# One load of x in 16 rows, a split of the last values, and four more key rows per part on VectorE in a decode attention kernel

## The chip, the cores and the metric

The kernel runs on one core of one Trainium2 chip. The metric is device time in microseconds (us) of one execution, here the median of three. A profiled execution gives, besides its own time, a span from the first to the last instruction; what lies around the span is launch and end.

The engines by the profile's names: PE (TensorE, matmuls; PEld is its weight loads), DVE (VectorE), ACT (ScalarE), POOL (GpSimd) and SP (SyncE, which here only issues DMAs). SBUF is the on-chip memory, PSUM the memory that matmuls write to. All DMAs of the core share 16 DMA engines.

## The reference

One token (x has 512 numbers) goes through a layer norm; its result is the input of an attention over a key and value cache with 32 heads of 128 and a window of the last 4096 positions, and of a small MLP. The MLP's silu gates the attention's output. With a sequence of one, the four shifted groups in the MLP (g0 to g3) are zero. Every head has its own keys and values, so the kernel reads 32 heads x 4096 positions x 128 numbers x 2 bytes = 32 MiB of keys and as much of values, once each.

```python
def _A_ref(x, k_cache, v_cache, wq, wo):        # 32 heads of 128, window W = 4096
    q = (x @ wq).reshape(B, Sq, Hq, Dh).transpose(0, 2, 1, 3)
    k = k_cache[:, :, Sk - W:, :]
    v = v_cache[:, :, Sk - W:, :]
    scores = jnp.einsum("bhqd,bhkd->bhqk", q, k) * (Dh ** -0.5)
    o = jnp.einsum("bhqk,bhkd->bhqd", softmax(scores), v)
    return o.transpose(0, 2, 1, 3).reshape(B, Sq, Hq * Dh) @ wo

xn = layernorm(A_x)
s = _A_ref(xn, A_k_cache, A_v_cache, A_wq, A_wo)
g = silu(_B_ref(xn, B_w1, B_w2, B_w3, B_w4))    # MLP with layer norm, gelu and residual
return A_x + s * g
```

## The kernel before

**Tiling.** The heads are worked in eight groups of G = 4. A group's keys (4 MB) fill one tile of 128 partitions x 128 rows x 128 numbers (CP = 128): partition p holds 128 positions of one of the four heads. A group's values lie in the same way. There are three buffers for keys and, once the weights' pool `wts` has been given back, two for values.

**DMA order.** SP issues nearly all loads, in program order and through one queue (q1 in the profile): w2, w3, w4, then keys of groups 0 (in two halves, rows 0 to 63 and 64 to 127), 1 and 2, values of group 0, keys of 3, values of 1, and so on. Blocks of wo are in between. An issue waits until the buffer that it fills is free, and what is behind it in SP's order waits too. The last group's values come in pieces (`cuts`, L528: rows 0 to 63, 64 to 95, 96 to 127), and after them the rows of wo of the last four heads, two heads at a time (L543 to L545). x and wq are issued by ACT, on a queue of their own (q10): x twice, as 128 partitions of 4 numbers (`x_bf`, L79) and as 4 rows of 128 on partitions 0, 32, 64 and 96 (`x_row`, L82).

**Start.** x_bf is cast (L183), the layer norm follows (L158 to L179, with two matmuls by ones and a POOL power), then q (L208) as soon as wq has landed, then its spreading over the partitions (`q_bc`, L216) and its transposes (`q_pair`, L225). The MLP (L228 to L280) runs beside it; its row form uses `xn_row` (L242), which is made from x_row, and ends in `g_row`. The PSUM pool `ps_misc` has one buffer, which all tiles of the tag "misc" use in turn.

**Scores.** Each group's 128 key rows are shared out (`nd`, L308). The first nd rows go to DVE in four equal parts (`k_vector`, L316: a product with q_bc, L321, and a sum over the 128 numbers, L323). The others are transposed by PE two rows at a time (`k_turn`, L339), copied from PSUM by ACT (L342) and multiplied with q_pair (`k_scores`, L350). nd is 80, but 64 in group 0 and in group 7.

**Softmax and values.** Maximum (`sm_max`, `sm_turn`), exponential with its sum (`sm_exp`, L388), then the product with the values, four rows in one matmul (`v_wide`, L427), copy (L433), transposes (`v_turn`, L444), sum (`v_add`, L450) and scaling by the denominator (`v_out`). These run two groups behind the keys (LAG = 2). PE, DVE and ACT have an order written out by hand in this loop (from L529); each runs its instructions in that order.

**End.** For the last group, rows 0 to 95 of the values go through v_wide, v_turn and v_add; v_add writes its sum to a PSUM tile `oT`, and the 32 matmuls of `v_part` (L461) add rows 96 to 127 to the same tile. L471 scales it, the 16 matmuls of `y_head` (L525, by L155: four for each head) apply the last four heads' rows of wo, L654 multiplies with g_row, L656 adds x_row, and the result goes out. `warm` (L506) issues matmuls on zeros whose result nobody reads.

Of the kernel before, what the change touches and what calls it, by code (L numbers as in the profile page):

```python
# [8 lines left out]
P = 128  # L9
BF16 = mybir.dt.bfloat16  # L10
FP32 = mybir.dt.float32
ACT = mybir.ActivationFunctionType
ALU = mybir.AluOpType
AX = mybir.AxisListType
# [4 lines left out]
G = 4  # L19
# [3 lines left out]
LATE = 7  # L23
# [3 lines left out]
def kernel(  # L27
# [14 lines left out]
    nc = tc.nc  # L42

    Bb, Sq, D = A_x.shape
# [30 lines left out]
    def load(dst, src):  # L75
        return tc.keep_in_program_order(nc.sync.dma_start(out=dst, in_=src))  # L76

    x_bf = small.tile([P, KC], BF16, name="x_bf")
    nc.scalar.dma_start(out=x_bf[:], in_=A_x.rearrange("a b (p c) -> p (a b c)", p=P))  # L79
    x_row = small.tile([P, P], BF16, name="x_row")  # L80
    nc.gpsimd.memset(x_row[:], 0.0)
    nc.scalar.dma_start(out=x_row[0:P:32, :], in_=A_x.rearrange("a b (j n) -> (a b j) n", j=KC))  # L82
    wq_sb = wts.tile([P, KC, HD], BF16, name="wq_sb")
    nc.scalar.dma_start(out=wq_sb[:].rearrange("p c n -> p (c n)"),
                        in_=A_wq.rearrange("(a b c) n -> b a (c n)", a=4, c=KC))
# [93 lines left out]
        return xc, negmean, rstd  # L179


    x_f = small.tile([P, KC], FP32, name="x_f")
    nc.vector.tensor_copy(out=x_f[:], in_=x_bf[:])  # L183
    xc, negmean, rstd = ln_stats(x_f[:], "x")
    xn_f = small.tile([P, KC], FP32, name="xn_f")
    nc.vector.tensor_scalar(out=xn_f[:], in0=xc[:], scalar1=rstd[:], scalar2=None, op0=ALU.mult)
# [51 lines left out]
    z3_bf = small.tile([P, KC], BF16, name="z3_bf")  # L238
    nc.vector.tensor_scalar(out=z3_bf[:], in0=xc3[:], scalar1=rstd3[:], scalar2=None, op0=ALU.mult)

    xn_row = small.tile([P, P], FP32, name="xn_row")
    nc.vector.tensor_scalar(out=xn_row[:], in0=x_row[:], scalar1=negmean[:], scalar2=rstd[:],  # L242
                            op0=ALU.add, op1=ALU.mult)
# [62 lines left out]
    st = {}  # L306

    def nd(g):  # L308
        return 64 if g == 0 or g >= LATE else 80

    def k_open(g):
        st[g] = {
# [101 lines left out]
    def load_rows(h, n):  # L414
        load(wo_rows[:, h - h_part:h - h_part + n, :],
             A_wo[h * P:(h + n) * P, :].rearrange("(h p) n -> p h n", p=P))
# [28 lines left out]

    def v_add(g):
        s = st[g]
        if g < NG - 1:
            s["oT"] = sm_pool.tile([P, G], FP32, tag="oT", name="oT")
        nc.vector.tensor_reduce(out=s["oT"][:], in_=s["ot"][:].rearrange("p (x m) -> p m x", m=32)[:, 0:G, :],  # L450
                                axis=AX.X, op=ALU.add)

    def v_open(g):
        st[g]["oT"] = ps_tr.tile([P, G], FP32, tag="pt", name="oT")
        nc.tensor.matmul(st[g]["oT"][:], lhsT=zero_bf[:], rhs=zero_bf[:, 0:G], start=True, stop=False,
                         skip_group_check=True)

    def v_part(g, v, c0, c1):
        s = st[g]
        for c in range(c0, c1):  # L460
            nc.tensor.matmul(s["oT"][:], lhsT=v[:, c, :], rhs=s["pT"][:, c, :], start=False,  # L461
                             stop=(c == CP - 1), skip_group_check=True)

    def v_out(g):
        h = G * g
        b = [i for i, (h0, _) in enumerate(blocks) if h >= h0][-1]
        if b not in o_blk:
            o_blk[b] = sm_pool.tile([P, blocks[b][1]], BF16, tag=f"o{b}", bufs=1, name="o")
        c = h - blocks[b][0]
        if g >= NG - 5:  # L470
            nc.vector.tensor_tensor(out=o_blk[b][:, c:c + G], in0=st[g]["oT"][:], in1=st[g]["rden"][:],  # L471
                                    op=ALU.mult)
            return
        for k in range(G):
            nc.scalar.mul(o_blk[b][:, c + k:c + k + 1], st[g]["oT"][:, k:k + 1], st[g]["rden"][:, k:k + 1])
# [49 lines left out]
        rows_add(y_ps, o_blk[3][:, h - h_part:h - h_part + 1], wo_row(h), h == H - 1)  # L525

    NG = H // G
    cuts = (0, 64, 96, CP)  # L528
    region = tc.manual_schedule(engines={mybir.EngineType.PE, mybir.EngineType.DVE,  # L529
                                         mybir.EngineType.Activation})  # L530
    region.__enter__()
# [1 line left out]
    for s in range(NG + LAG):  # L533
# [7 lines left out]
            wo_rows = v_pool.tile([P, H - h_part, D], BF16, tag="wo_rows", bufs=1, name="wo_rows")  # L541
        if last:
            v = load_kv(v_pool, A_v_cache, h, cuts)  # L543
            for r in (H - G, H - 2):
                load_rows(r, 2)  # L545
        elif h >= 0:
            v = load_kv(v_pool, A_v_cache, h)
        if h == 3:
# [7 lines left out]
        if s < NG:  # L556
            nb = len(batches(s))

            def keys(b0, b1):
                for b in range(b0, b1):  # L560
                    k_turn(s, kn, b)
                    if b > 0:
                        k_scores(s, b - 1)

            k_open(s)
            k_vector(s, kn, 0)
            keys(0, 2)
            if s == 7:
                v_turn(h - 1)
                v_add(h - 1)  # L570
                v_out(h - 1)
            elif s > 1:
                sm_den(s - 2)
                sm_rden(s - 2)
            elif s == 1:
                sm_max(0)
            k_vector(s, kn, 1)
            keys(2, 4)
            if s == 7:
                sm_den(h)  # L580
                sm_rden(h)
                keys(4, nb - 2)
                sm_turn(s - 1)
                keys(nb - 2, nb)
            else:
                if s > 0:
                    sm_turn(s - 1)
                keys(4, nb)
            k_scores(s, nb - 1)
            sm_own(s)  # L590
            if s == 7:
                k_vector(s, kn, 2)
                v_wide(h, v)
                sm_exp(s - 1)
                v_turn(h)
                y_open()
                k_vector(s, kn, 3)
                v_add(h)
                v_out(h)
                ox_spread(1)  # L600
                sm_max(s)
                continue
            if s > 0:
                sm_exp(s - 1)
            if h > 0:
                v_turn(h - 1)
            k_vector(s, kn, 2)
            if h >= 0:
                v_wide(h, v)
            if h > 0:  # L610
                v_add(h - 1)
                v_out(h - 1)
            if s == 6:
                ox_spread(0)
            k_vector(s, kn, 3)
            if s == 6:
                ox_pick(0)
            if s > 0:
                sm_max(s)
        elif s == NG:  # L620
            ox_pick(1)
            sm_turn(NG - 1)
            sm_exp(NG - 1)
            y_wide(1, False)
            sm_den(NG - 2)
            sm_rden(NG - 2)
            y_wide(0, False)
            warm(3)
            v_wide(h, v)
            sm_den(NG - 1)  # L630
            sm_rden(NG - 1)
            v_turn(h)
            v_add(h)
            v_out(h)
            ox_spread(2)
        else:
            v_open(h)
            warm(2)
            v_wide(h, v, cuts[1], last=False)
            ox_pick(2, 1)  # L640
            y_wide(2, True)
            nc.scalar.copy(out=y_sum[:], in_=yr[0][:].rearrange("p j n -> p (j n)"))
            v_wide(h, v, cuts[2], cuts[1])
            warm(2)
            v_turn(h)
            v_add(h)
            rows_add(y_ps, ind, y_sum, False)
            v_part(h, v, cuts[2], CP)
            v_out(h)
            for r in range(H - G, H):  # L650
                y_head(r)
# [36 lines left out]
```

## Time and profile before

| what | before |
|---|---|
| three runs, us | 193.21, 193.31, 193.57 (median 193.31) |
| profiled execution, us | 193.37 |
| its span, us | 191.2 |
| PE, DVE, ACT busy in the span, us | 121.2, 150.9, 89.5 |
| read from HBM, MB | 78.84, 412 GB/s over the span |
| DMA engines' time by q1, q10, q8 (code) | 91.6%, 5.1%, 0.3% |
| granted PE clock, mean | 0.704 |
| x_bf: issue, landing | 0.74, 4.77 |
| wq: matmuls start | 19.87 |
| first DVE product on keys (group 0, group 1) | 25.93, 42.08 |
| last issue of keys, first matmul on them | 130.42, 153.51 |
| output DMA issued | 188.71 |

Times inside an execution are us from the start of its span. A row of the profile's list of groups names line, engine, operation, tiles, shapes and how often it ran, then busy us and mean ns, and behind the last bar the idle time of that engine just before it and what ended that. The chain of waits is followed back from the last instruction: each piece is the work, or the DMA, that released the next one. The windows give, for a stretch of time, the busy time (and instructions) of PE, PEld, DVE, ACT and POOL, the granted PE clock, the mean busy share of the 16 DMA engines, and GB/s. The trace also holds a record of every DMA packet and of every landing (a DMA has landed when all 16 engines have reported).

### The profile page before, as it was taken

What the parts mean: (1) busy time and instruction counts of PE and PEld (TensorE: products, weight loads), DVE (VectorE), ACT (ScalarE), POOL (GpSimd) and SP (SyncE); (2) the same over time, 40 slices, a digit from 0 to 9 for tenths busy, and PEclk for the clock granted to TensorE, in tenths of its full rate; (3) what the DMA queues carried; (4) which work ended last, traced back from release to release, by engine and by line L of the source; (5) the groups of instructions that cost most, each with busy time, mean ns of one, the idle gap of its engine ahead of it and who ended that gap; (6) DMA issues with size and microseconds to landing.
All of it is one profiled execution on the core that took longest, in us unless ns stands there. A gap on an engine that the chain in (4) does not pass through costs nothing.

```text
span 191.2 us, 2843 instructions
## 1 busy us (share of the span) xinstructions
PE 121.2 (63%) x1161; PEld 77.0 (40%) x1161; DVE 150.9 (79%) x175; ACT 89.5 (47%) x191; POOL 2.4 (1%) x11
## 2 busy tenths in 40 slices
PE   1554853989826368356945773681889289749772
PEld 0430222767615334243434432540764078513321
DVE  1560169979999999999999999999999997990111
ACT  2001270887795076527364654552575147743120
POOL 2110000000000000000000000000000000000000
PEclk9999696555665556955585579558555855996999
DMA  6999999999999999999999999999999998999990
GB/s 202 436 444 410 431 425 432 439 439 437 432 440 432 432 428 439 439 439 418 428 418 425 439 428 408 456 432 435 439 439 434 428 432 379 471 435 394 415 372 29
DMA packets 4572, 79.02 MB, mean 413 GB/s; under 512 B 624, under 2 KB 1232, under 8 KB 1488
## 3 DMA queue, kind: packets, MB, share of 16 engines
q1 hardware_dynamic: 4264, 74.65, 91.6%
q10 hardware_dynamic: 296, 4.20, 5.1%
q8 instruction: 9, 0.15, 0.3%
q14 instruction: 3, 0.02, 0.0%
HBM read 78.84 MB, written 0.00 MB: 412 GB/s over the span
## 4 chain that ended last, share of the span: by engine, by line
DVE 47%; DMA 42%; PE 6%; ACT 1%; issue 1%; SPq 1%; DVEq 0%; ACTq 0%
DMA kv<-in_A_k_cache_dram 31%; DVE S L323 28%; DVE prod L321 16%; DMA kv<-in_A_v_cache_dram 9%; PE pt L339 3%; DMA x_bf<-in_A_x_dram 2%; ACT kt L342 1%; PE ov L427 1%; PE sT L350 1%; DVE m L366 1%; SPq L76 1%; DVE S L364 1%; DVE mx L374 1%; PE oT L461 1%; PE ot_ps L444 0%
## 5 line engine op out<-in xcount | busy, mean ns | idle before, releaser
L323 DVE TENSOR_REDUCE S<-prod 128x20 f32<-128x2560 bf16 (+1 forms) x32 | 86.0, 2686 | 1.1
L342 ACT COPY kt<-pt 128x1024 bf16<-128x1024 bf16 x52 | 51.4, 1013 | 40.0 <-PE pt L339 38.1
L339 PE MATMUL pt<-ident_f,kv 128*128 128x128 f32 x208 | 49.2, 392 | 10.0 <-DMA kv<-in_A_k_cache_dram 10.0
L321 DVE TENSOR_TENSOR prod<-kv,q_bc 128x2560 bf16<-128x2560 bf16 (+1 forms) x32 | 45.4, 1417 | 3.6 <-ACT q_pair L225 1.8
L339 PEld LDWEIGHTS pt<-ident_f,kv 128*128 128x128 f32 x208 | 36.2, 205 | 13.9 <-DMA kv<-in_A_k_cache_dram 9.3
L350 PE MATMUL sT<-q_pair,kt 128*128 128x8 bf16 x416 | 19.6, 170 | 14.9 <-ACT kt L342 14.8
L350 PEld LDWEIGHTS <-kt 128*128 128x128 bf16 x416 | 16.9, 105 | 26.1 <-ACT kt L342 24.9
L427 PE MATMUL ov<-kv,pT 128*16 128x512 bf16 x248 | 23.2, 536 | 1.2 <-DMA kv<-in_A_v_cache_dram 1.2
L388 ACT ACTIVATE pT<-S,mb 128x128 bf16<-128x128 f32 x32 | 13.9, 572 | 0.3
L372 PE MATMUL mt_ps<-ident_f,m 128*1 128x128 f32 x8 | 2.9, 360 | 16.6 <-DVE rden L399 16.1
L433 ACT COPY ov_sb<-ov 128x512 f32<-128x512 f32 x8 | 4.7, 586 | 18.4 <-PE ov L427 18.4
L427 PEld LDWEIGHTS <-pT 128*16 128x16 bf16 x248 | 6.9, 112 | 14.3 <-issue 12.7
L359 ACT ACTIVATE own<-sT,par 128x48 f32<-128x48 f32 (+1 forms) x32 | 7.5, 356 | 3.7 <-PE sT L350 3.7
L444 PE MATMUL ot_ps<-ident_f,ov_sb 128*128 128x128 f32 x32 | 7.5, 379 | 2.2 <-ACT mb L384 1.7
L211 DVE CAST q_row<-qr_ps 128x512 bf16<-128x512 f32 x1 | 0.7, 692 | 10.0 <-PE qr_ps L208 10.0
L388 ACT ACTIVATION_READ_ACCUMULATOR pT<-S,mb 128x1 f32 x32 | 8.3, 258 | 0.0
L372 PEld LDWEIGHTS mt_ps<-ident_f,m 128*1 128x1 f32 x8 | 0.6, 80 | 17.1 <-DVE rden L399 16.4
L399 DVE RECIPROCAL rden<-den_ps 128x4 f32<-128x4 f32 x8 | 1.4, 175 | 6.7 <-PE den_ps L394 6.7
L381 PE MATMUL mb_ps<-md,par_t 5*128 5x4 f32 x16 | 3.9, 311 | 4.1 <-DVE md L376 4.1
L255 ACT ACTIVATE a_row<-a_ps 128x384 bf16<-128x384 f32 x1 | 0.5, 491 | 12.1 <-remote 12.1
L444 PEld LDWEIGHTS ot_ps<-ident_f,ov_sb 128*128 128x128 f32 x32 | 4.8, 188 | 3.2 <-ACT mb L384 2.1
L208 PE MATMUL qr_ps<-wq_sb,xq_bf 128*1 128x512 bf16 x32 | 3.5, 611 | 3.6 <-DMA wq_sb<-in_A_wq_dram 3.6
(122 smaller groups left out, 82.8 us busy)
## 6 DMA issues: line engine op xcount, KB each, us to landing
kv<-in_A_k_cache_dram SPq DMA_DIRECT2D x7, 4096.0 KB, 31.0
kv<-in_A_v_cache_dram SPq DMA_DIRECT2D x7, 4096.0 KB, 30.6
wq_sb<-in_A_wq_dram ACTq DMA_DIRECT2D x1, 4096.0 KB, 17.5
kv<-in_A_k_cache_dram SPq DMA_DIRECT2D x2, 2048.0 KB, 27.5
wo<-in_A_wo_dram SPq DMA_DIRECT2D x1, 2048.0 KB
kv<-in_A_v_cache_dram SPq DMA_DIRECT2D x1, 2048.0 KB
kv<-in_A_v_cache_dram SPq DMA_DIRECT2D x2, 1024.0 KB, 16.3
w_sb<-in_B_w_dram SPq DMA_DIRECT2D x1, 1376.0 KB, 10.3
```

Of the source, the lines that this page charges most:

```text
L208: nc.tensor.matmul(qr[b][32 * a:32 * a + 1], lhsT=xq_bf[:, c:c + 1], rhs=wc[:, 4 * b:4 * b + 4, a, :], start=False, stop=(c == KC - 1), sk ...
L321: nc.vector.tensor_tensor(out=prod[:, 0:m, :], in0=kn[:, rows, :], in1=q_bc[:, g:g + 1, :].to_broadcast([P, m, Dh]), op=ALU.mult)
L323: nc.vector.tensor_reduce(out=st[g]["S"][:, rows], in_=prod[:, 0:m, :], axis=AX.X, op=ALU.add)
L339: nc.tensor.transpose(pt[:, i, :], kn[:, c:c + 2, :].rearrange("p c d -> p (c d)").bitcast(FP32), ident_f[:])
L342: nc.scalar.copy(out=kts[b][:, 0:n, :], in_=pt[:, 0:n, :].bitcast(BF16))
L350: nc.tensor.matmul(st[g]["sT"][:, c:c + 2, :].rearrange("p c a -> p (c a)"), lhsT=kt[:, i, l::2], rhs=q_pair[:, g, l, :], start=(l == 0), ...
L359: nc.scalar.mul(s["own"][:, 0:m, a], s["sT"][:, 0:m, a], par[:, a:a + 1])
L381: nc.tensor.matmul(mb_ps[:], lhsT=par_t[:].rearrange("k b a -> k (b a)"), rhs=md[:], start=True, stop=True)
L388: nc.scalar.activation(out=s["pT"][:, :, a], in_=s["S"][:], func=ACT.Exp, scale=scale, bias=mb[:, a:a + 1], accum_out=s["sum"][:, a:a + 1])
L427: nc.tensor.matmul(ov[r:r + 4 * G], lhsT=s["pT"][:, c:c + 4, :].rearrange("p i a -> p (i a)"), rhs=v[:, c:c + 4, :], start=(i < 4), stop=( ...
L433: nc.scalar.copy(out=s["ov_sb"][:], in_=ov[:])
L444: nc.tensor.transpose(ot_ps[:, step * j:step * j + P], s["ov_sb"][:, j, :], ident_f[:])
```

## The change

1. x is loaded once, as 16 rows of 32 numbers (`x_in`). Both forms are made of it on chip: a matmul with a 0/1 matrix (`x_up`) copies every row to its 8 partitions, a mask (`x_own`) and a sum pick each partition's 4 numbers (`x_f`); for x_row the rows are spread by a mask (`r_in`), and a matmul with another 0/1 matrix (`r_up`) puts them together. These are 2 small matmuls and 9 small DVE instructions, in place of a cast on DVE, a memset on POOL and two DMAs (one remains).
2. In group 0, 76 key rows go to DVE rather than 64, in parts of 19 rather than 16.
3. The last 32 rows of the last values come in two halves. The matmuls on them add up in a PSUM tile of their own (`oP`); v_add's sum goes to SBUF, and one more DVE instruction (`both`) adds the two. In PE's order, the matmul rows of y_sum and the first half's 16 matmuls now stand ahead of the transposes of v_turn, and the second half's 16 behind; one call of warm(2) is gone.
4. The last four heads' rows of wo come as three heads and one, not two and two.

```diff
-    x_bf = small.tile([P, KC], BF16, name="x_bf")
-    nc.scalar.dma_start(out=x_bf[:], in_=A_x.rearrange("a b (p c) -> p (a b c)", p=P))
-    x_row = small.tile([P, P], BF16, name="x_row")
-    nc.gpsimd.memset(x_row[:], 0.0)
-    nc.scalar.dma_start(out=x_row[0:P:32, :], in_=A_x.rearrange("a b (j n) -> (a b j) n", j=KC))
+    XR, XC = 16, D // 16
+    x_in = small.tile([XR, XC], BF16, name="x_in")
+    nc.scalar.dma_start(out=x_in[:], in_=A_x.rearrange("a b (r n) -> (a b r) n", r=XR))
...
+    m8 = P // XR
+    x_up = wts.tile([XR, XR, m8], BF16, name="x_up")
+    nc.vector.tensor_copy(out=x_up[:], in_=ident_bf[0:XR, 0:XR].unsqueeze(2).to_broadcast([XR, XR, m8]))
+    x_own = wts.tile([P, m8], BF16, name="x_own")
+    nc.vector.tensor_reduce(out=x_own[:], in_=ident_bf[:].rearrange("d (i t) -> d t i", t=m8), axis=AX.X, op=ALU.max)
+    x_all = ps_misc.tile([P, m8, KC], FP32, tag="misc", name="x_all")
+    nc.tensor.matmul(x_all[:].rearrange("p t c -> p (t c)"), lhsT=x_up[:].rearrange("k r t -> k (r t)"), rhs=x_in[:],
+                     start=True, stop=True)
+    x_pick = wts.tile([P, m8, KC], FP32, name="x_pick")
+    nc.vector.tensor_tensor(out=x_pick[:], in0=x_all[:], in1=x_own[:].unsqueeze(2).to_broadcast([P, m8, KC]), op=ALU.mult)
     x_f = small.tile([P, KC], FP32, name="x_f")
-    nc.vector.tensor_copy(out=x_f[:], in_=x_bf[:])
+    nc.vector.tensor_reduce(out=x_f[:], in_=x_pick[:].rearrange("p t c -> p c t"), axis=AX.X, op=ALU.add)
...
+    r_slot = wts.tile([XR, KC], BF16, name="r_slot")
+    nc.vector.tensor_reduce(out=r_slot[:], in_=ident_bf[0:XR, 0:XR].rearrange("k (j a) -> k a j", a=KC), axis=AX.X, op=ALU.max)
+    r_row = wts.tile([XR, KC], BF16, name="r_row")
+    nc.vector.tensor_reduce(out=r_row[:], in_=ident_bf[0:XR, 0:XR].rearrange("k (j a) -> k j a", a=KC), axis=AX.X, op=ALU.max)
+    r_up = wts.tile([XR, KC, PB], BF16, name="r_up")
+    nc.vector.tensor_copy(out=r_up[:], in_=r_row[:].unsqueeze(2).to_broadcast([XR, KC, PB]))
+    r_in = wts.tile([XR, KC, XC], BF16, name="r_in")
+    nc.vector.tensor_tensor(out=r_in[:], in0=x_in[:].unsqueeze(1).to_broadcast([XR, KC, XC]),
+                            in1=r_slot[:].unsqueeze(2).to_broadcast([XR, KC, XC]), op=ALU.mult)
+    xr_ps = ps_misc.tile([P, P], FP32, tag="misc", name="xr_ps")
+    nc.tensor.matmul(xr_ps[:], lhsT=r_up[:].rearrange("k j b -> k (j b)"), rhs=r_in[:].rearrange("k a n -> k (a n)"),
+                     start=True, stop=True)
+    x_row = small.tile([P, P], BF16, name="x_row")
+    nc.vector.tensor_copy(out=x_row[:], in_=xr_ps[:])
...
     def nd(g):
-        return 64 if g == 0 or g >= LATE else 80
+        return 76 if g == 0 else 64 if g >= LATE else 80
...
     def v_add(g):
         s = st[g]
-        if g < NG - 1:
-            s["oT"] = sm_pool.tile([P, G], FP32, tag="oT", name="oT")
+        s["oT"] = sm_pool.tile([P, G], FP32, tag="oT", name="oT")
...
     def v_open(g):
-        st[g]["oT"] = ps_tr.tile([P, G], FP32, tag="pt", name="oT")
-        nc.tensor.matmul(st[g]["oT"][:], lhsT=zero_bf[:], rhs=zero_bf[:, 0:G], start=True, stop=False,
+        st[g]["oP"] = ps_tr.tile([P, G], FP32, tag="pt", name="oP")
+        nc.tensor.matmul(st[g]["oP"][:], lhsT=zero_bf[:], rhs=zero_bf[:, 0:G], start=True, stop=False,
                          skip_group_check=True)
...
+        if g == NG - 1:
+            both = sm_pool.tile([P, G], FP32, tag="both", bufs=1, name="both")
+            nc.vector.tensor_tensor(out=both[:], in0=st[g]["oP"][:], in1=st[g]["oT"][:], op=ALU.add)
+            st[g]["oT"] = both
...
-    cuts = (0, 64, 96, CP)
+    cuts = (0, 64, 96, 112, CP)
...
-            for r in (H - G, H - 2):
-                load_rows(r, 2)
+            load_rows(H - G, G - 1)
+            load_rows(H - 1, 1)
...
             v_wide(h, v, cuts[2], cuts[1])
-            warm(2)
+            rows_add(y_ps, ind, y_sum, False)
+            v_part(h, v, cuts[2], cuts[3])
             v_turn(h)
             v_add(h)
-            rows_add(y_ps, ind, y_sum, False)
-            v_part(h, v, cuts[2], CP)
+            v_part(h, v, cuts[3], CP)
             v_out(h)
```

More of the change, by code (lines that the diff above doesn't have):

```diff
@@ L460, in v_part @@
         for c in range(c0, c1):
-            nc.tensor.matmul(s["oT"][:], lhsT=v[:, c, :], rhs=s["pT"][:, c, :], start=False,
+            nc.tensor.matmul(s["oP"][:], lhsT=v[:, c, :], rhs=s["pT"][:, c, :], start=False,
                              stop=(c == CP - 1), skip_group_check=True)
```

## The prediction

> **What bounds the kernel now.** First the page's 40 slices, then the chain of waits, the windows of the last microseconds, and the rows of each operation.
>
> ```profile
> DMA  6999999999999999999999999999999998999990
> GB/s 202 436 444 410 431 425 432 439 439 437 432 440 432 432 428 439 439 439 418 428 418 425 439 428 408 456 432 435 439 439 434 428 432 379 471 435 394 415 372 29
> ...
> q8 instruction: 9, 0.15, 0.3%
> ...
> DVE 47%; DMA 42%; PE 6%; ACT 1%; issue 1%; SPq 1%; DVEq 0%; ACTq 0%
> ```
>
> The chain puts VectorE (DVE) first, but the DMA row is full from the second slice to the last but one. 78.84 MB at some 435 GB/s take 181 us of the 191.2 us span. DVE stands in the chain because it frees key buffers: the load of the last keys is issued at 130.42, when DVE has read an old buffer, and lands at 153.47. By the landings in the trace the queue still held work up to 143.7 at that moment, so an issue a few us later starts no byte later. I read the kernel as one DMA stream with a tail; a step counts if it changes the stream or the tail.
>
> The tail, in the chain:
>
> ```profile
> 168.94 17.25 DMA kv<-in_A_v_cache_dram
> ...
> 186.24 0.97 PE oT L461 x32
> ...
> 187.23 0.17 DVE o L471
> ...
> 187.45 0.59 PE y_ps L155 x16
> ...
> 188.06 0.30 DVE y L654
> ```
>
> The last values land, 32 matmuls (L461) finish their sum, DVE scales it, 16 matmuls (L155) apply the last four heads' rows of wo. But those 16 did not run through. The weight loads of that line in the timeline from 187.6 on, and the answer on the rows' tile:
>
> ```profile
> 187.73 0.10 PEld L155 LDWEIGHTS <-o 128*1 128x1 bf16 x7
> ...
> L76 SPq DMA_DIRECT2D wo_rows<-in_A_wo_dram x2: 469/531/593, 169.6 to 170.2; - x2
> ...
> DMA to landing us min/median/max: 17.3/17.4/17.5
> ```
>
> The second pair of rows was issued at 170.2 and landed 17.5 us later, at 187.7. The first 8 matmuls start by 187.51, the other 8 from 187.73. So the landing of wo_rows, not the values' sum, releases the end, and any byte ahead of it counts.
>
> ```profile
> 183.50:185.50 2.00, 1.58 (x14) 0.64 (x13) 0.00 (x0) 1.10 (x2) 0.00 (x0) 1.00 0.99 398
> 185.50:186.00 0.50, 0.50 (x11) 0.11 (x8) 0.23 (x1) 0.00 (x0) 0.00 (x0) 1.00 0.54 193
> 186.00:186.50 0.50, 0.32 (x14) 0.27 (x11) 0.00 (x0) 0.00 (x0) 0.00 (x0) 1.00 0.65 227
> 186.50:187.00 0.50, 0.50 (x26) 0.50 (x23) 0.00 (x0) 0.00 (x0) 0.00 (x0) 1.00 0.54 193
> 187.00:187.50 0.50, 0.25 (x12) 0.16 (x13) 0.16 (x1) 0.00 (x0) 0.00 (x0) 1.00 0.19 55
> ```
>
> The last two columns (DMA share, GB/s) fall to half from 185.5: some DMA engines are done, others work until 187.2. The packet records say why: a 32 KB packet takes 1.213 us, but the one after an instruction packet (the q8 row: 16 KB, some 1.07 us) takes 1.7, so its engine falls behind by about 1.55 us. Eight such packets lie inside the stream and land on different engines; these end last. The ninth starts at 187.213, right behind the last packet of the last engine (187.207), and that engine's landing came 0.48 us after its last packet, where the other late ones needed 0.29 to 0.35. I read 0.13 us of the end as that collision. In "Runtime: NRT & Kernel Launch", section "Instruction fetch mechanics", the Trainium skill says that an engine's sequencer fetches code itself in blocks of 256 instructions, with the cost mostly hidden; the records agree on the block (16 KB, one per some 130 PE pairs of load and matmul), but here it is not hidden, since DMA is the bound.
>
> **The change, part by part** (us of the span).
>
> *x once.* Now x_bf is 128 packets of 8 bytes, 8 per DMA engine, each holding its engine 15 ns (9 and a gap of 6): 0.12. x_row is four packets and one DMA more: 0.02. The new load is 16 packets, one per engine. Stream: -0.12. A larger gain is not excluded: w2's first 8 packets per engine take until 4.23, 2.45 from the first packet at 1.78, while a first packet of 1.0 and seven of 0.165 make 2.16; so -0.29 is the far bound, and 0 the near one. I take -0.12, the packets' own time. The chain names x_bf (issue 0.74, landing 4.77) because the second half of the first keys is issued behind it; that half's bytes start moving only at 20 or later, so an earlier issue is worth nothing.
>
> x_f now comes through a matmul (0.16, as L194), a product (0.21, L494) and a reduce (0.27, L498) in place of a cast of 0.17: 0.5 more, hidden by the wait for wq: xq_bf is ready at 9.05, wq at 19.87. Without that cover, +0.5. The masks x_up and x_own (0.26 and 0.38 by L192 and L136) run before x lands. Of the five row operations on DVE each lies between 0.16 (L188) and 0.41 (the pick of 256), 0.8 to 2.1 together; DVE idles 10.0 before q_row (L211). xr_ps shares the one "misc" buffer: behind it wait a_ps's zeros, at most 0.9, before w3's matmuls.
>
> wq's issue starts 1.1 earlier (x_row's 1.09 is gone). wq then shares the engines with w3 from the start, packet by packet, so w3, and with it a_ps (2.93, ahead of q on TensorE), comes later: q ends between 1.1 earlier and 0.7 later. Up to 0.5 of the earliness is lost anyway, because DVE's first product starts at 25.93 and the first keys land at 25.83. V's first issue (30.98) waits for hr; the queue has work until 51.
>
> *76 rows on DVE.* Bound by DVE's own rows:
>
> ```profile
> L323 DVE TENSOR_REDUCE S<-prod 128x20 f32<-128x2560 bf16 x24 | 67.7, 2820 | 0.8
> L321 DVE TENSOR_TENSOR prod<-kv,q_bc 128x2560 bf16<-128x2560 bf16 x24 | 35.6, 1483 | 1.7 <-DMA kv<-in_A_k_cache_dram 1.6
> L323 DVE TENSOR_REDUCE S<-prod 128x16 f32<-128x2048 bf16 x8 | 18.3, 2285 | 0.2
> L321 DVE TENSOR_TENSOR prod<-kv,q_bc 128x2048 bf16<-128x2048 bf16 x8 | 9.8, 1219 | 1.9 <-ACT q_pair L225 1.8
> ...
> 42.08 1.49 DVE L321 TENSOR_TENSOR prod<-kv,q_bc 128x2560 bf16<-128x2560 bf16 x1 [1.32 <-DMA kv<-in_A_k_cache_dram]
> ...
> 162.58 0.28 DVE L374 TENSOR_REDUCE mx<-mt_ps 1x4 f32<-1x128 f32 x1 [1.15 <-PE mt_ps L372]
> ```
>
> A row costs (1483-1219+2820-2285)/4 = 200 ns, twelve cost 2.4. The idle 1.32 before the second keys takes part, so DVE is about 1.1 late from 42 (up to 1.8 with a late q). It gets 0.33 back at 134.12 (waiting for keys) and 1.15 at 162.58 (waiting for TensorE). Its later releases delay issues at 57, 76, 94, 112 and 130, each with 10 to 20 us of work queued. Cost 0; without all that cover +2.4. ScalarE saves one copy of eight (1.0), TensorE 6 transposes and 12 score matmuls: worth nothing in time, but 18 pairs fewer in TensorE's code.
>
> *Last values in two halves.* Each DMA engine moves 16 packets of 4 KB (0.159) in place of 8 of 8 KB (0.309), with gaps of 6 ns and one semaphore packet: +0.13 of stream. SP issues one DMA more (0.55, ending at 171.2), while those bytes have their turn from 183 on. In the tail L461 has 16 matmuls behind the last landing instead of 32 (25 ns apart): -0.40; `both` adds one DVE step of 0.20. So o is ready 0.20 earlier, 187.25 for TensorE: hidden, since wo_rows decides; without that cover -0.2. The transposes (0.66) now follow the first half's 16 matmuls (landing near 185.0) and end at about 186.1, just before the last landing at 186.2. The two warm matmuls' place is taken by y_sum's rows.
>
> *Three heads and one.* The same bytes; behind the last landing stand 4 matmuls, not 8: -0.06 (187.79 to 187.73 for the last start). Three heads land 0.35 earlier, about 187.2, in time for o.
>
> *The ninth code fetch.* 18 pairs fewer and the two new matmuls against the two warm ones: the fetch comes some 18 pairs later, among the last 16 matmuls, behind the end of the stream: -0.13, or 0 if my reading of the 0.48 is wrong. I take -0.13.
>
> Sum: -0.12 +0.13 -0.06 -0.13 = -0.18. The profiled run took 193.37 (span 191.2, 2.17 around it), so 193.19; the median of the three runs, 193.31, lies 0.06 lower: **193.13**.
>
> **Rivals.** *The clock.* "TensorE: Matmul & The Clock Gate" of the Trainium skill (section "Part 1: The HAM clock gate") says that activity in a window of about 3.4 us releases the throttle and idleness brings it back; the page's PEclk agrees (0.50 in 173.7 to 177.0, 1.00 after). Two warm matmuls (0.6) go, so the tail could run at half clock: four transposes take 1.12 at half (125.53) against 0.66, the second half then starts 0.36 late, o is ready 0.15 after before's: 193.4. Against: from 180.6 to 183.8 TensorE works 1.8 of 3.2, unchanged, and keeps 1.00. 7%.
>
> *The first loads bring the stream forward.* If the chain were right that x_bf holds up the keys, the stream would move by x's earlier landing, 1.3 to 2: about 191.7. Against: the DMA row is full. 6%. A better start within the -0.29 bound gives 192.96; 15%.
>
> *DVE becomes the bound (slower).* If the 1.1 of lateness at 42 reaches the issue at 130.42 and with it the last keys' landing, as the chain links them, the time is 193.31 + 1.1 = 194.4. For it: DVE has 47% of the chain and no gap from 42 to 133. It decides once the lateness uses up the queue, some 10 us at 130, or exceeds the 1.48 of later waits and the tail's 0.78 (TensorE waits that long for values at 181.35). 8%.
>
> *x or the fetch brings nothing:* 193.25 to 193.4, in the forecast's own range.
>
> **How the numbers follow.** Forecast 64%, with its own range 192.9 to 193.45. This kernel's measurement tells 0.2% (0.39) from nothing: faster means below 192.92, slower above 193.70. Faster: the 6% of a moved stream, a third of the better start (5%), 6% of the forecast's lower edge: 17%. Slower: DVE's 8% and 3% for a code fetch that meets a late engine: 11%. Same: 72%. The range takes the bounds of the unknown terms and some noise (the three runs differ by 0.36): 192.75 to 193.6.
>
> **What would show it.** Right: the DMA row still full; the last landings within 0.15 of 186.19 (values) and between 187.5 and 187.7 (rows); the last four of the 16 matmuls apart from the first twelve; o near 187.2; DVE late at the second keys, no longer so after 162. Wrong: a last landing more than 0.4 away, or y waiting for o rather than for rows.

## The result and the profile after

Fifteen runs of the changed kernel gave a median of 193.65 us (193.33 to 194.04); fifteen runs of the kernel before on the same chip gave 193.34 (193.19 to 193.57). The ratio is 1.0016, with a 95% interval of 1.0008 to 1.0023: some 0.3 us slower, where 193.13 was forecast, and just above the forecast's range (192.75 to 193.6). The profiled execution took 193.84. Its span is 192.1, 0.9 longer than before's; around the span lie 1.82 (median of the runs) where before has 2.17. Two sizes that the prediction took as fixed have moved, in opposite directions.

The changed kernel's page, the lines that answer to those of before:

```profile
DMA  6999999999999999999999999999999999999990
GB/s 217 449 402 434 409 423 449 437 430 423 433 432 437 437 430 433 437 437 437 433 416 423 416 440 399 447 437 430 433 430 425 437 437 386 471 430 396 403 359 25
...
q8 instruction: 9, 0.15, 0.3%
...
DVE 55%; DMA 33%; PE 6%; SPq 2%; ACT 1%; issue 1%; ACTq 0%; DVEq 0%
```

The DMA row is full as before, now up to the last slice but one. The commonest figure of the GB/s row is 437, where in before it was 439: the same bytes, a little slower. VectorE's larger share of the chain means nothing for the end, as the chain's tail shows:

```profile
170.62 17.46 DMA wo_rows<-in_A_wo_dram
188.12 0.76 PE y_ps L153 x15
188.90 0.30 DVE y L679
```

Rows of wo set the end, as in before, but y comes at 188.90 where before had 188.06. The timeline of the same microseconds (start, duration, engine, line):

```profile
187.09 0.56 PE L482 MATMUL oP<-pT,kv 128*128 128x4 bf16 x16 [0.23 <-DMA kv<-in_A_v_cache_dram]
...
187.88 0.16 DVE L496 TENSOR_TENSOR o<-both,rden 128x4 bf16<-128x4 f32 x1
...
188.58 0.09 PEld L153 LDWEIGHTS <-o 128*1 128x1 bf16 x3 [0.16 <-issue]
```

The last values land at 187.045 by the trace's landing records, against 186.188 in before; the last rows at 188.531, against 187.685. The whole end of the stream comes 0.85 later. The tail itself has the form that the change gives it: 16 matmuls, one more VectorE step, 12 matmuls on three heads' rows, and the fourth head's apart from them.

### The profile page after: what moved, and what is told of

Same layout as the page of the kernel before. It is cut to its first block, busy times and chain, and to the rows that moved or that the text cites. A ratio compares the mean times of both kernels' runs of the same rounds, so it can differ in the third digit from the quotient of the medians.

```text
span 192.1 us, 2819 instructions
## 1 busy us (share of the span) xinstructions
PE 119.8 (62%) x1143; PEld 76.3 (40%) x1143; DVE 154.9 (81%) x184; ACT 89.3 (47%) x191; POOL 2.2 (1%) x10
## 4 chain that ended last, share of the span: by engine, by line
DVE 55%; DMA 33%; PE 6%; SPq 2%; ACT 1%; issue 1%; ACTq 0%; DVEq 0%
DVE S L345 33%; DMA kv<-in_A_k_cache_dram 24%; DVE prod L343 18%; DMA wo_rows<-in_A_wo_dram 9%; PE pt L361 3%; SPq L76 2%; ACT kt L364 1%; PE ov L449 1%; PE sT L372 1%; DVE m L388 1%; DVE S L386 1%; DVE mx L396 1%; PE ot_ps L466 0%; DVE md L398 0%; PE y_ps L153 0%
## 5 line engine op out<-in xcount | busy, mean ns | idle before, releaser
L345 DVE TENSOR_REDUCE S<-prod 128x20 f32<-128x2560 bf16 (+2 forms) x32 | 87.6, 2737 | 1.1
L364 ACT COPY kt<-pt 128x1024 bf16<-128x1024 bf16 (+1 forms) x51 | 50.0, 1004 | 45.6 <-PE pt L361 43.9
L361 PE MATMUL pt<-ident_f,kv 128*128 128x128 f32 x202 | 48.0, 392 | 8.5 <-DMA kv<-in_A_k_cache_dram 8.5
L343 DVE TENSOR_TENSOR prod<-kv,q_bc 128x2560 bf16<-128x2560 bf16 (+2 forms) x32 | 46.1, 1442 | 3.5 <-DMA kv<-in_A_k_cache_dram 3.3
L361 PEld LDWEIGHTS pt<-ident_f,kv 128*128 128x128 f32 x202 | 35.2, 205 | 12.3 <-DMA kv<-in_A_k_cache_dram 9.8
L449 PE MATMUL ov<-kv,pT 128*16 128x512 bf16 x248 | 22.6, 525 | 0.9 <-DMA kv<-in_A_v_cache_dram 0.9
L381 ACT ACTIVATE own<-sT,par 128x48 f32<-128x48 f32 (+2 forms) x32 | 7.5, 352 | 3.7 <-PE sT L372 3.7
L218 ACT CAST q_row<-qr_ps 128x512 bf16<-128x512 f32 x1 | 0.6, 585 | 16.7 <-PE qr_ps L216 16.7
L403 PEld LDWEIGHTS mb_ps<-md,par_t 5*128 5x128 f32 x16 | 3.8, 290 | 6.4 <-PE sT L372 5.0
```

The lines of the kernel that those rows point to most:

```text
L343: nc.vector.tensor_tensor(out=prod[:, 0:m, :], in0=kn[:, rows, :], in1=q_bc[:, g:g + 1, :].to_broadcast([P, m, Dh]), op=ALU.mult)
L345: nc.vector.tensor_reduce(out=st[g]["S"][:, rows], in_=prod[:, 0:m, :], axis=AX.X, op=ALU.add)
L361: nc.tensor.transpose(pt[:, i, :], kn[:, c:c + 2, :].rearrange("p c d -> p (c d)").bitcast(FP32), ident_f[:])
L364: nc.scalar.copy(out=kts[b][:, 0:n, :], in_=pt[:, 0:n, :].bitcast(BF16))
L381: nc.scalar.mul(s["own"][:, 0:m, a], s["sT"][:, 0:m, a], par[:, a:a + 1])
L403: nc.tensor.matmul(mb_ps[:], lhsT=par_t[:].rearrange("k b a -> k (b a)"), rhs=md[:], start=True, stop=True)
```

## The experiments

The page names no operation that is slower. The trace's packet records do: a 32 KB packet of values, 1213 ns in before (91 of 96 packets in the middle of the first load of values), takes most often 1215 and next 1222 in the changed kernel, and smaller packets lose as much: 16 KB 611.7 to 614.8, 8 KB 309.0 to 313.2, 4 KB 159.0 to 161.8, 1 KB 46.0 to 48.0 ns (averages from 25 us on, without the packets that are over 30% longer than the usual one). Most of the bytes belong to loads that the change does not touch. What is changed for values and weights is where they are written. x_in takes 64 bytes a partition where x_bf took a slot of 32, and `both` another 32, so every tile allocated behind them lies 64 bytes further on: the tiles for values began at byte 160000 of each partition (625 x 256) and now begin at 160064; so too the weights. An unused tile `pad` (L71, 192 bytes) had put them on a multiple of 256. The keys' tiles lie ahead of x, 128 bytes past a multiple of 256 in both kernels.

Theory A: a tile that is off a multiple of 256 bytes costs each of its packets a few ns, and that is the loss. Theory B: the loss is in the start, where the first keys' packets took longer in the changed kernel. Theory C: the new tail costs it.

**e1, the kernel before, tiles moved by 64 bytes; e8, by 128.** The edit of e1; e8 has 160 in place of 128.

```diff
-    small.tile([P, 96], BF16, name="pad")
+    small.tile([P, 128], BF16, name="pad")
```

> The kernel before with one unused tile grown by 64 bytes per partition, so that all tiles behind it in SBUF, the values' and wo's among them, start 64 bytes past a multiple of 256 bytes, as in the changed kernel; nothing else differs. Theory A (the change's slowness is the place of the tiles in SBUF: in its trace a full values packet takes 1216 to 1217 ns, in that of before 1213): 193.55 to 193.75, values packets at 1216 to 1217 ns. Theory B (the loss is at the start, where the first packet of the first keys takes 850 ns in place of 611 on each engine) and theory C (the loss is in the tail's four pieces): 193.3, packets at 1213.

> The kernel before with all tiles behind one unused tile moved by 128 bytes, so that values and wo start 128 bytes past a multiple of 256, where the keys' tiles lie in all these kernels. If only multiples of 256 bytes are free of the loss: 194.0 to 194.2, values packets at 1216 to 1217 ns. If multiples of 128 or 64 bytes are enough: 193.35, and 1213 ns.

Measured: e1 194.16 (194.11 to 194.24), before beside it 193.38, ratio 1.0043 [1.0030, 1.0057]; e8 194.06 (193.81 to 194.17) against 193.29, ratio 1.0037 [1.0025, 1.0049]. No instruction of these kernels differs from before's, and both lose 0.8 us. In e1's chain of waits the tail of before stands 0.87 later:

```profile
169.80 17.26 DMA kv<-in_A_v_cache_dram
187.11 0.97 PE oT L461 x32
```

The last values land at 187.064. Of the 0.88 by which that is late, 0.22 is there when the second half of the first keys lands, and 0.65 comes after it, a little with every load. Added up over e1's packets from 30 us on, the longer times make an estimated 0.54 us for each of the 16 engines, most of the 0.65.

**e2, the whole change with `pad` cut to 128 bytes**, so that values and weights stand on a multiple of 256 again.

```diff
-    small.tile([P, 96], BF16, name="pad")
+    small.tile([P, 64], BF16, name="pad")
```

> The changed kernel with that unused tile made 64 bytes smaller, so that values and wo start at multiples of 256 bytes again, as before. Theory A: 193.25 to 193.4, packets back at 1213 ns. Theories B and C: 193.65 as the changed kernel.

Measured: 192.82 (192.68 to 192.95), ratio to before 0.9974 [0.9965, 0.9984]. The change with its tiles on their old places is 0.83 faster than as it came, and 0.56 faster than before; 0.36 of the 0.56 lies around the span (1.80 beside 2.16), 0.2 inside (median 191.0 beside 191.2). e2's chain:

```profile
170.37 15.82 DMA kv<-in_A_v_cache_dram
186.24 0.57 PE oP L482 x16
187.24 0.56 PE y_ps L153 x16
187.82 0.30 DVE y L679
```

The values land where before had them (186.191), the rows at 187.503. The chain follows the values and draws the 16 matmuls of y_ps as one piece, but their records show the first twelve starting from 187.244 to 187.364 and the last four from 187.545, right behind the rows' landing: the rows still set the end, by 0.13. Theory A holds for values and weights. B and C remain as possible smaller terms, and e3 to e7 take the change apart with the tiles in place.

**e3, the tail alone (last values in two halves; rows of three heads and one); e4, the start alone (x once; 76 rows).** Each has the change's lines for these parts, and `pad` at 160 bytes, which keeps the tiles on 160000.

```diff
-    small.tile([P, 96], BF16, name="pad")
+    small.tile([P, 80], BF16, name="pad")
...
-    cuts = (0, 64, 96, CP)
+    cuts = (0, 64, 96, 112, CP)
...
-            for r in (H - G, H - 2):
-                load_rows(r, 2)
+            load_rows(H - G, G - 1)
+            load_rows(H - 1, 1)
```

```diff
-    small.tile([P, 96], BF16, name="pad")
+    small.tile([P, 80], BF16, name="pad")
...
+    x_in = small.tile([XR, XC], BF16, name="x_in")
...
-        return 64 if g == 0 or g >= LATE else 80
+        return 76 if g == 0 else 64 if g >= LATE else 80
```

> Parts 3 and 4 of the change alone (last values in two halves, three heads and one) on the kernel before, with values and wo at multiples of 256 bytes. By the forecast's terms: +0.13 of stream, -0.06 behind the last rows: about 193.4 (193.2 without the collision at the last landing). Theory C: 193.55 or more. Theories A and B: 193.2 to 193.4.

> Parts 1 and 2 of the change alone (one load of x, 76 rows on VectorE) on the kernel before, with values and wo at multiples of 256 bytes. By the forecast's terms: -0.12: 193.2. Theory A: 193.2 to 193.35. Theory B: 193.5 to 193.65, with the first packets of the first keys at some 850 ns. VectorE late at the second keys by 1 us or less, and no longer behind after 162.

Measured: e3 193.19 (192.93 to 193.42), 0.9993 [0.9984, 1.0001]; e4 192.94 (192.86 to 193.31), 0.9979 [0.9970, 0.9988]. By their spans they hardly differ from before (median 191.3 and 191.1 beside 191.2); the time around the span is 1.90 and 1.80, where before beside them has 2.16. What both gain lies mostly outside their spans. C falls as the cause of the 0.83: e3 has the whole tail, and its span is 0.1 longer than before's.

**e5, x once alone; e6, 76 rows alone; e7, the split of the values alone**, each again with values and weights where before has them. Their lines are those of the two diffs above, one part at a time: `pad` at 160 bytes with x_in (e5), nd alone with `pad` as in before (e6), `pad` at 160 bytes with cuts, oP and both (e7).

> Part 1 alone (one load of x), values and wo at multiples of 256 bytes. The forecast's term: -0.12, bounds 0 and -0.29: 193.1 to 193.35. Parts 1 and 2 together gave 192.94, with 1.80 us around the span where the kernel before has 2.16. If part 1 makes that shorter time around the span: 192.85 to 193.05 and 1.80; if part 2 does: 193.2 to 193.35 and 2.16.

> Part 2 alone (76 key rows of the first group on VectorE); no tile moves. The forecast: 0, that is 193.35, with VectorE 1.1 us late at the second keys and no longer behind after 162. If VectorE sets the time: 194.4. If this part shortens the time around the span (2.16 before): 193.0.

> Part 3 alone (the last 32 rows of values in two halves with a sum of their own), values and wo at multiples of 256 bytes. The forecast's term of +0.13 of stream alone: 193.45 to 193.5. If the parts 3 and 4 gained their 0.19 around the span rather than in it: 193.1 to 193.25, with some 1.9 around the span and the last landings 0.1 later than in the kernel before.

Measured, beside 193.29 of before: e5 193.76 (193.52 to 194.12), 1.0026 [1.0017, 1.0034]; e6 193.15 with a wide spread (192.66 to 194.13), 0.9995 [0.9981, 1.0010]; e7 193.25 (193.02 to 193.63), 0.9994 [0.9984, 1.0004]. In e7 too the time around the span is shorter (1.91 beside 2.16); its span is 0.3 longer (191.4 beside 191.1). e5 was a surprise: slower alone than together with the 76 rows in e4. Its stream is not late (the last rows land at 187.450), and the output is issued at 188.75, as in before (188.71). But it lands at 191.314, 2.57 later, where before needed 1.67. The windows of e5 around the store (the last two columns are the DMA engines' busy share and GB/s):

```profile
189.50:190.00 0.50, 0.00 (x0) 0.00 (x0) 0.00 (x0) 0.00 (x0) 0.00 (x0) 0.50 0.05 16
190.00:190.50 0.50, 0.00 (x0) 0.00 (x0) 0.00 (x0) 0.00 (x0) 0.00 (x0) 0.50 0.01 2
```

An output of 1 KB can't make 16 GB/s in half a microsecond, 8 KB. It is a packet of 8 KB of an instruction queue (q14) from 189.905 to 190.323. The store's last packet began at 190.319, when the others had been done for 0.26 us, and its landing followed 0.99 later, against 0.35 in before. The wait of that packet explains 0.26; why its landing then took 0.64 longer is not shown.

B falls with these kernels. The excess time of the packets in the first half of the first keys, over 611 ns each, is 0.28 us for each DMA engine in the changed kernel; it is 0.17 in e4, which is not slow, and 0.19 in e1, which has no x part.

**e11, e5 with six more clears on VectorE; e10, before with them.** The clears write the same zeros again. If that packet is VectorE's code, a longer VectorE program moves it. The six clears also test what set the time around the span.

```diff
     nc.vector.memset(zero_bf[:], 0.0)
+    for _ in range(6):
+        nc.vector.memset(zero_bf[:], 0.0)
```

> The x part alone, as e5, with the same six clears on VectorE at the start. e5 was 193.76, and in its profile a packet of 8 KB of the instruction queue began at 189.905, among the output's packets, and the output landed 0.93 later than in before. If that fetch is VectorE's code and its place is what e5 lost by, the packet now comes some us earlier, the output lands 1.6 to 1.7 after its issue, and the median is 192.8 to 193.0. If e5 lost by its stream or by x itself, it stays at 193.6 to 193.9.

> The kernel before with six more clears of a small tile on VectorE at the start, so that every later VectorE instruction stands six places further on in its program; nothing moves in SBUF. The stream is that of before: last values at 186.2, span 191.0 to 191.3. If the time around the span depends on where VectorE's program ends, it falls from 2.16 to 1.8 to 1.9 and the median is 193.0; if it depends on another engine's, it stays 2.16 and the median is 193.3. Should VectorE's code now be fetched during the store of the output, the span is 0.5 to 1.0 longer, and a packet of the instruction queue shows it after 188.7.

Measured, beside 193.38: e11 192.99 (192.82 to 193.47), 0.9980 [0.9971, 0.9988]; e10 192.92 (192.62 to 193.29), 0.9978 [0.9969, 0.9986]. In e11 the instruction queue's packet comes at 170.22, the output lands 1.67 after its issue, and e5's windows look like this:

```profile
189.50:190.00 0.50, 0.00 (x0) 0.00 (x0) 0.00 (x0) 0.00 (x0) 0.00 (x0) 0.95 0.01 2
```

More instructions made e5 0.77 faster. Its loss was the place of a code fetch. An early q14 packet tells whose code it is: it comes at 47.0 in before, 45.8 with two more TensorE matmuls (e12), 31.4 with six more VectorE instructions (e10), and at 29.9 in e5 and 13.0 in e11. In all five VectorE had by then started 58 to 64 instructions of its program, while ScalarE had started 5 to 38. And the kernel before, with six useless clears, gains 0.46: its span hardly moves (median 191.1 beside 191.2), the time around it falls from 2.18 to 1.79.

**e12, before with two more idle matmuls; e13, before with two more small copies on ScalarE.**

```diff
-            warm(3)
+            warm(5)
```

```diff
         nc.scalar.copy(out=mb[:], in_=mb_ps[:])
+        if g == 0:
+            for _ in range(2):
+                nc.scalar.copy(out=mb[:], in_=mb_ps[:])
```

> The kernel before with five in place of three of the idle matmuls at the start of the last values but one: TensorE's program is two matmuls longer, nothing else changes. All kernels whose time around the span fell to 1.8 to 1.9 have another number of TensorE matmuls than before, and all that kept 2.16 have before's. If that is what sets it, it falls to 1.8 to 1.9 and the median is 192.9 to 193.05; else it stays 2.16 and the median is 193.3 within 0.1.

> The kernel before with two more copies of a 128x4 tile on ScalarE in the first softmax, some 0.5 us of ScalarE at a place where it has room; VectorE's and TensorE's programs are as before. Six more instructions on VectorE took the time around the span from 2.18 to 1.79, two more on TensorE left it at 2.19. If ScalarE's program counts as VectorE's does, the time around the span is 1.75 to 1.95 and the median 192.9 to 193.1; if VectorE's alone counts, it stays at 2.1 to 2.3 and the median is 193.3 within 0.15.

Measured: e12 193.45 (193.19 to 194.39) beside 193.38, 1.0010 [0.9998, 1.0023], with 2.19 around the span; e13 193.27 (193.11 to 193.89) beside 193.29, 1.0002 [0.9993, 1.0010], with 2.17. So six more instructions on VectorE moved it, and two more on TensorE or on ScalarE did not; six on those were not tried. The number of VectorE's instructions is not the whole of it: e6 executes as many there as before (175), with 18 matmuls and one ScalarE copy fewer, and has 1.85. One thing goes with the shorter time: a last q14 packet of 8 KB after 160 us, between 163.29 (e6) and 192.88 (e10, behind the span). Nine of the eleven kernels with the shorter time have it (e3 and e7, at 1.90 and 1.91, do not), and none of the six with the longer. How the program's layout sets 1.8 or 2.17 was not found.

**e9, the whole change with the keys too on a multiple of 256; e14, the same for the kernel before; e15, e14 with the six clears.**

```diff
+    kpad_pool = ctx.enter_context(tc.tile_pool(name="kpad", bufs=1))
+    kpad_pool.tile([P, 64], BF16, name="kpad")
     k_pool = ctx.enter_context(tc.tile_pool(name="k", bufs=K_BUFS))
...
-    small.tile([P, 96], BF16, name="pad")
```

e14 and e15 keep 64 bytes of `pad`, so that values and weights stay on a multiple of 256.

> The whole change, with an unused tile of 128 bytes ahead of the key tiles and without the tile named pad: now the key tiles too, which lie 128 bytes past a multiple of 256 in every kernel so far, start on a multiple of 256, and values and weights stay on one, as in e2. If any tile off a multiple of 256 bytes costs its packets some 4 ns, the second, third and seventh loads of keys (32 KB packets of 1217 ns on average in before and in e2) fall to 1213 ns, the last values land 0.05 to 0.12 us earlier than in e2, and the median is 192.6 to 192.8. If those three loads are slow for another reason (what is loaded or issued beside them), they stay at 1217 and the median is that of e2, 192.82 within 0.1.

> The kernel before with the unused 128 bytes ahead of the key tiles and the tile named pad cut to 64 bytes: keys, values and weights all on multiples of 256 bytes, no instruction changed. By the place of tiles every load runs at 1213 ns a packet, and the last values, which landed at 186.19 in before and at 185.70 in e9, land at 185.7 to 185.9. If the stream still sets the end, the median falls by 0.3 to 0.5, to 192.9 to 193.05, with 2.17 around the span; if TensorE or VectorE has become the bound, as the profile of e9 shows it, less of it arrives: 193.1 to 193.4, with a wide spread.

> e14 with the six clears of e10: all tiles on multiples of 256 bytes and VectorE's program six instructions longer, none of the four parts of the change. If the two gains add up, the median is that of e14 less 0.35 to 0.45: 192.5 to 192.9, as low as the whole change on its old places (e2, 192.82) without any of its parts. If it is 193.0 or more, the gains do not add up.

The packets do as theory A says: the three loads of keys that averaged 1217 ns in before and e2 now run at 1213 (in the second load of e9, 95 of 96 packets at exactly 1213). From the landing of the first keys' second half to that of the last values the stream of e14 takes 153.80 us, before's 153.92. The time follows only in part. e14: 193.13 beside 193.29, 1.0008 [0.9983, 1.0033], an interval that one run at 195.86 of the eleven has widened. Its chain has before's form, earlier by 0.31, most of it from the start of this one execution:

```profile
168.57 17.31 DMA kv<-in_A_v_cache_dram
185.93 0.97 PE oT L463 x32
```

e15: 192.71 (192.53 to 193.68), 0.9977 [0.9965, 0.9990], 0.4 below e14, with 1.82 around the span. It has none of the four parts of the change, and the lowest median of all kernels here. That the two gains add up is not shown: e14's own gain lies within its interval, and e15's ratio is that of e10 (0.9978), which has the clears alone.

e9: 193.16 (192.53 to 193.92), 0.9985 [0.9971, 0.9999], above e2 where less was expected. In its profile the last values landed at 185.699, 0.49 before e2's (0.36 of it already there at the first keys), but TensorE was not there to use them:

```profile
185.77 0.56 PE L483 MATMUL oP<-pT,kv 128*128 128x4 bf16 x16
...
186.18 0.64 PE L467 MATMUL ot_ps<-ident_f,ov_sb 128*128 128x128 f32 x4
...
186.66 0.55 PE L483 MATMUL oP<-pT,kv 128*128 128x4 bf16 x16
```

No line names a DMA as the releaser: TensorE works one piece after the other, and the last 16 matmuls start 0.96 after their values are there. Its clock was granted less in the stretch before: it stayed at 0.50 until 179.86, in e2 until 178.19. The windows from 175 to 180, e9 first, then e2 (the clock is the third column from the end):

```profile
175.00:180.00 5.00, 5.00 (x41) 1.39 (x44) 0.18 (x1) 0.76 (x4) 0.00 (x0) 0.51 0.98 416
```

```profile
175.00:180.00 5.00, 5.00 (x50) 1.44 (x41) 0.00 (x0) 0.17 (x1) 0.00 (x0) 0.68 0.92 390
```

TensorE is busy through all of both; at 0.51 it did 41 matmuls where 0.68 gave 50. That accounts for the profiled execution (193.12). Five of the twelve runs took 192.53 to 192.77; whether the others lost in this way was not seen, and the mean granted clock does not tell them apart (0.668 to 0.697 in the five, 0.659 to 0.696 in the seven).

## Why the prediction was wrong

Step by step, by the sum -0.18 on a profiled 193.37.

**The packet times (the step that failed).** The prediction took packets at before's 1.213, 0.309 and 0.159 us, and so put the loads that the change leaves alone at nothing, without a word on where they are written. The change moved their tiles, and the rows no longer held. The missing term is +0.83 (193.65 less 192.82; e1 gives 0.78 without any other edit), larger than all terms of the sum together, and no rival had it. The diff showed it: a tile of another size ahead of others, beside an unused tile named pad. "How a descriptor splits into AXI transactions" in the Trainium skill's page "DMA: Bandwidth & Descriptors" says that a descriptor that does not begin at a multiple of 256 bytes has its first transaction begin at the boundary below, and that the unused bytes cost beats of 32 bytes. That section speaks of the bytes that are read; here the side that is written is off. At the 27 bytes a ns of a packet here (32 KB in 1213 ns), 64 unused bytes would be an estimated 2.4 ns, 128 bytes 4.7. The traces agree in size, and only in part: with 64, 1215 in place of 1213 is the commonest time of the values' packets, but 1222 mostly the next; with 128 (e8), 1218 is clearly the commonest in the last two whole loads of values, while in the others 1213 is about as common. In before, the keys of groups 3 to 5, also 128 bytes off, lost nothing. Why the place costs time is thus not shown; that it does, is.

**The time around the span (failed, to the other side).** 2.17 was carried over as a constant. It fell by 0.35, and e10 shows that a longer VectorE program is enough for that. With this and the first term the sum is -0.18 + 0.83 - 0.35 = +0.30 on 193.37: 193.67, or 193.61 less the prediction's 0.06 from the profiled run to the median, beside 193.65 measured. That the rest of the sum fits is partly luck, since its own terms were met only in part, as follows.

**x once, -0.12.** Not seen as time: e11 has the same median span as before (191.2), and its time around the span is 0.41 shorter. The start did come forward: x_in lands at 3.62 (x_bf: 4.77), wq at 18.68 (19.83). In the changed kernel q then ran early and at full clock:

```profile
18.72 1.90 PE L216 MATMUL qr_ps<-wq_sb,xq_bf 128*1 128x512 bf16 x32 [1.96 <-DMA wq_sb<-in_A_wq_dram]
```

Before needed 3.45 for these 32, at a granted clock of 0.50 from 20.05 on, where the changed kernel has 1.00 from 17.24 to 27.48. So q ended 2.70 earlier, outside the forecast's bounds (1.1 earlier to 0.7 later). It was worth nothing, as forecast: the first product on the keys started only at 26.08, waiting for keys that landed at 25.99. w3 landed at 13.81, against 11.45: the sharing with wq is there too.

**76 rows, 0.** The lateness was right in size and in where it is made good; VectorE in the changed kernel:

```profile
43.35 1.49 DVE L343 TENSOR_TENSOR prod<-kv,q_bc 128x2560 bf16<-128x2560 bf16 x1
...
134.93 1.48 DVE L343 TENSOR_TENSOR prod<-kv,q_bc 128x2560 bf16<-128x2560 bf16 x1
...
162.97 0.28 DVE L396 TENSOR_REDUCE mx<-mt_ps 1x4 f32<-1x128 f32 x1 [0.73 <-PE mt_ps L394]
```

1.27 late at the second keys (1.1 was forecast), 0.81 at 134.93 without a wait for keys, 0.39 at the maximum, in a stream that is late itself. It never reached the last keys: the rival "DVE becomes the bound" (194.4) did not come about. e6's spread stays unexplained.

**Last values in two halves, +0.13; three heads and one, -0.06.** The totals of e7 and e3 cannot tell, because their time around the span fell by 0.25 and 0.26; their spans are 0.3 and 0.1 longer. In the stream the +0.13 is not seen: from the first keys' second half to the last values e7 takes 154.07 and e3 153.96, where before, e10, e12 and e13, with all loads as in before, take 153.92 to 154.12. The 0.06 is there in e2, where y starts 0.32 after the last rows' landing, against 0.37 in before. It was lost in the changed kernel: y starts 0.37 after the last rows' landing, as in before, with 4 matmuls instead of 8. The clock had gone down while TensorE waited for the late rows:

```profile
187.50:188.00 0.50, 0.15 (x6) 0.06 (x3) 0.28 (x2) 0.00 (x0) 0.00 (x0) 0.91 0.44 131
188.00:188.50 0.50, 0.38 (x12) 0.31 (x13) 0.05 (x1) 0.00 (x0) 0.00 (x0) 0.50 0.06 16
```

**The ninth code fetch, -0.13 (failed).** It was to come behind the end of the stream. It came at 187.941, again right behind the last packet of the last engine (187.935), whose landing took 0.60 after that packet, against 0.48. In before, the changed kernel, e2, e9 and e14 alike it comes when all but the last 16 matmuls have begun: with 18 pairs fewer in the program it moved with the program's end. The price was read rightly: in the seven traces where the fetch starts within 10 ns of the last engine's last packet, the last landing comes 0.42 to 0.60 after that packet; in the ten others 0.28 to 0.35, but for e8 (0.43). In e2 the fetch came 0.21 ahead of that packet, and the rows landed 0.28 after it. No term had it there, so for e2 that part of the gain is luck.

**The other rivals.** A stream brought forward by x (191.7) did not come: the DMA row is full and its end later. The tail's clock, feared without the two warm matmuls, was 1.00 until 187.9, so the four transposes took 0.64 us.

**The signs named** for the profile after: the DMA row full, the last four matmuls apart, VectorE late at the second keys and nearly made good by 162, all there; values at 186.19, rows at 187.5 to 187.7, o near 187.2, all three wrong by 0.7 to 0.9 in the changed kernel, and right in e2 (186.191, 187.503, and o from 187.03 to 187.20). The prediction's own test, a last landing more than 0.4 away, pointed at the failed step.

## What to carry to other kernels

When a change alters the size of any on-chip tile, work out the addresses of all tiles behind it before costing a DMA-bound stream: here 64 bytes cost 0.8 us, more than the four edits could bring. An unused tile in such a kernel may be there for its size alone. Under half a microsecond, test a gain against a kernel that has only the side effects (program length, tile places): before with six idle clears (192.92, ratio 0.9978) and with tile places besides (192.71, 0.9977) did about as well as the whole change in its best place (192.82, 0.9974).

## What the runs showed of the hardware

Writing values and weights 64 or 128 bytes off a multiple of 256 cost a packet some 2 to 5 ns on average whatever its size, so that small packets lose the larger share (4 KB: 159.0 to 161.8; 32 KB: 1214.1 to 1216.8). It is not simply additive: the keys of groups 3 to 5, at 128 past a multiple, ran at 1213 in before, among loads of values on a multiple, and at 1217 on average in the changed kernel, among loads off it. Why was not settled.

The time around the span has two values, 2.16 to 2.19 (before, e1, e8, e12, e13, e14) and 1.77 to 1.91 (all others, the changed kernel among them). Six more instructions on VectorE are enough to change it, but e6 changed it without any; the mechanism is open.

An 8 KB packet of VectorE's code that meets the store of the output at the very end cost 0.77 us (e5 against e11). "Instruction fetch mechanics" in the page "Runtime: NRT & Kernel Launch" of the Trainium skill speaks of blocks of 16 KiB, where VectorE's packets here have 8 KB, and calls the cost of crossing into one mostly hidden; at this place it is not. Six more instructions on VectorE (e11, packet at 170.22) or the 76 rows (e4, 174.21) moved it away.
